# One key buffer with the global keys woven in: window scores as 32 matmuls of 128 columns instead of 64 of 64, with a new order of operations

## The chip, the core and the metric

The kernel runs on one core of one Trainium2 chip. TensorE (PE) multiplies, with its weight loads shown apart as PEld; VectorE (DVE), ScalarE (ACT) and GpSimd (POOL) do the elementwise work; SyncE (SP) issues almost all DMAs. The metric is device time in microseconds (us), the median of several executions.

## The reference

Local and global attention for 8 batches of 8 heads, then a feed-forward network whose activation is h - tanh(h). Everything is float32.

```python
s_g   = scale * q_g @ k_all.T                 # 32 global queries see all 32 + 512 keys
out_g = softmax(s_g) @ v_all
s_ll  = scale * q_l @ k_l.T                   # 512 local queries, head_dim 64
s_ll  = where(abs(i - j) <= 32, s_ll, -1e9)   # a window of 32 to each side
s_lg  = scale * q_l @ k_g.T                   # and all 32 global keys
out_l = softmax([s_lg, s_ll]) @ [v_g, v_l]
x     = concat(out_g, out_l)                  # (8 * 544, 512)
h     = x @ w_in                              # 512 -> 2048
out   = (h - tanh(h)) @ w_out                 # 2048 -> 512
```

The window is cut into blocks of 32 positions: a block of 32 queries needs its own key block, its two neighbours and the 32 global keys, together 128 keys.

## The kernel before

Heads go in pairs (rows 0 to 63 and 64 to 127 of the partitions). Pairs 0 to 7 (batches 0 and 1) use an older scheme (`Pair`). Pairs 8 to 31 (batches 2 to 7, 24 pairs) use `WindowPair`, which the change touches. Each feed-forward product is three float32r products (high x high, high x low, low x high), 512 columns each: hidden steps at L1176 and output steps at L1224, 12 matmuls each; they make up most of PE's work, and attention is threaded between them. The last batch's feed-forward work has a form of its own (L1550, L1576, L1670).

For one window pair the steps are these, with the line of the instruction. Keys and queries come by 8 DMAs (L838) in a form that DVE's 32x32 transposes turn (L842 keys, L845 queries). `scores` (L867) does, for each of 16 blocks and 2 heads, two matmuls of 64 columns: one on the first two key blocks, one on the third key block and the global keys, which lie behind the 512 local columns of the same buffer, `win_kw` (its tile is printed as `first_m`). A float32 matmul is two records in the profile, each with a weight load, so a visit of `scores` shows 128 matmul records. `global_scores` (L889) takes the global queries against all keys, with 8 matmuls of 128 columns and 8 of 64, in all 32 records. Then DVE takes maxima (L967), ACT does the exponentials (L975), POOL the normalization (L989), and DVE turns the probabilities into keys-by-queries (L1007, L956). `product` (L1037, 56 records) multiplies them with the values, which SP has loaded as window slices: four DMAs per pair (L1085, L1086), each window's 96 local rows above the 32 global rows. The product is split into a high and a low part (L368 CAST to `x_hi`, L1070 to `x_lo`) for the feed-forward network.

One visit on PE glues the products of pair j to the scores of pair j+1. The global scores of a pair stand ahead of its scores in time: right after the scores of pair j+1 the buffer `win_kw` is free, DVE turns the keys of pair j+2 into it, and L889 of pair j+2 follows.

The order on every engine is not written out: `Order.run` is a list scheduler that plays the program with durations of its own and picks the operation that can start first, with due times and penalties from the table `CFG`; where an operation may run on two engines (`either`: DVE or ACT), the table's penalties decide. In gaps that it foresees between 5 and 72 us it puts matmuls with no use (`fill`, L1832).

## Time and profile before

| | us |
|---|---|
| median of 3 runs | 943.48 |
| lowest and highest run | 943.43 and 944.66 |
| span of the profiled execution, first to last instruction | 942.0 |
| PE busy in it | 922.5 (98%) |
| DVE, ACT, POOL busy in it | 702.5, 367.2, 342.8 |

The profile is read from PE outwards: with PE busy for 98% of the span, an edit counts by what it takes from PE's own sequence or from the few places where PE stands still. Until about 58 us PE does only attention of the first batch, then both kinds of work, from 184 us the window pairs between feed-forward steps, and from about 811 us the last feed-forward work alone. Busy time of PE hides short losses, because the ends of matmuls are modelled; so the start times in the timeline are read as well.

### The profile page before, as it was taken

The page shows a single profiled execution, that of the slowest core. Times are in us where ns is not written, and L with a number is a line of the kernel's source. Part 1 is how long each engine was busy: PE and PEld are TensorE (multiplying, and loading weights), DVE is VectorE, ACT ScalarE, POOL GpSimd, SP SyncE. Part 2 cuts the span into 40 slices and gives each one's busy share as a digit, 9 for nine tenths or more (in the row PEclk, how much of TensorE's full clock was granted, in tenths as well). Part 3 has the DMA queues.
Part 4 walks back from the last instruction along what each step waited for, and adds up shares of the span by engine and source line. Part 5 has one row for each costly group of instructions (what it writes and reads, how often), then busy time and mean ns, then how long its engine had stood idle before and what let it go on. Part 6 is the DMA issues. An engine that isn't in the chain of part 4 may idle for free.

```text
span 942.0 us, 24357 instructions
## 1 busy us (share of the span) xinstructions
PE 922.5 (98%) x9387; PEld 754.8 (80%) x9387; DVE 702.5 (75%) x2281; ACT 367.2 (39%) x1075; POOL 342.8 (36%) x573
## 2 busy tenths in 40 slices
PE   8989999999999999999999999999999999999998
PEld 5667777778878888888788888888878888899896
DVE  6997565597878876888677778886877786878773
ACT  6976656433334122332324222332223222533232
POOL 4677655543333333334324243333333233110000
PEclk9999999999999999999999999999999999999999
DMA  9565244542344224342424323343434210100001
GB/s 233 151 184 166 85 129 101 96 94 43 69 84 98 55 42 73 70 101 49 78 46 114 57 34 59 74 97 58 74 63 100 49 28 14 46 1 1 1 1 67
DMA packets 243571, 70.25 MB, mean 75 GB/s; under 512 B 228096, under 2 KB 236800, under 8 KB 243456
## 3 DMA queue, kind: packets, MB, share of 16 engines
q1 hardware_dynamic: 242112, 68.19, 33.0%
q8 instruction: 73, 1.20, 0.6%
q10 hardware_dynamic: 1344, 0.52, 0.2%
q14 instruction: 42, 0.34, 0.1%
HBM read 59.77 MB, written 8.91 MB: 73 GB/s over the span
## 4 chain that ended last, share of the span: by engine, by line
PE 91%; DVE 3%; ACT 2%; issue 1%; POOL 1%; DMA 1%; ACTq 0%; POOLq 0%; SPq 0%; DVEq 0%
PE bank L1224 33%; PE bank L1176 32%; PE bank L1550 7%; PE bank L1670 5%; PE bank L1037 5%; PE bank L867 4%; PE bank L889 1%; PE bank L641 1%; PE bank L1576 1%; PE bank L738 1%; DMA first_raw<-in_k_l_dram 1%; PE bank L545 1%; POOL wraw L779 0%; DMA first_raw<-in_q_l_dram 0%; PE bank L661 0%
## 5 line engine op out<-in xcount | busy, mean ns | idle before, releaser
L1193 POOL TENSOR_TENSOR glo<-t,ghi 128x512 fp32r<-128x512 f32 x112 | 145.7, 1301 | 286.0 <-PE bank L1224 192.8
L1007 DVE STREAM_TRANSPOSE keys_first<-prob 32x256 f32<-32x256 f32 x384 | 167.3, 436 | 10.3 <-POOL prob L989 4.0
L1184 ACT ACTIVATE t<-bank 128x512 f32<-128x512 f32 x112 | 66.7, 596 | 226.9 <-PE bank L1176 223.7
L1187 DVE TENSOR_TENSOR t<-bank,t 128x512 f32<-128x512 f32 x112 | 76.8, 688 | 70.2 <-ACT t L1184 69.0
L1224 PE MATMUL bank<-w_out_hi,ghi 128*128 128x512 f32 x448 | 127.2, 397 | 0.2
L1224 PE MATMUL bank<-w_out_hi,glo 128*128 128x512 f32 x448 | 125.4, 394 | 0.0
L1224 PE MATMUL bank<-w_out_lo,ghi 128*128 128x512 f32 x448 | 125.0, 393 | 0.3 <-POOL w_out_lo L451 0.3
L1176 PE MATMUL bank<-x_hi,w_in_hi 128*128 128x512 f32 x448 | 121.7, 393 | 0.3 <-DVE x_hi L368 0.3
L1176 PE MATMUL bank<-x_hi,w_in_lo 128*128 128x512 f32 x448 | 120.4, 391 | 0.0
L1176 PE MATMUL bank<-x_lo,w_in_hi 128*128 128x512 f32 x448 | 120.2, 390 | 0.0
L975 ACT ACTIVATE prob<-prob,st 128x128 f32<-128x128 f32 x192 | 74.5, 391 | 92.1 <-DVE st L967 92.1
L1224 PEld LDWEIGHTS bank<-w_out_hi,ghi 128*128 128x128 f32 x448 | 82.5, 188 | 20.7 <-ACT wpair L368 1.2
L1176 PEld LDWEIGHTS bank<-x_hi,w_in_hi 128*128 128x128 f32 x448 | 83.1, 188 | 19.9 <-issue 1.0
L1176 PEld LDWEIGHTS bank<-x_lo,w_in_hi 128*128 128x128 f32 x448 | 83.9, 188 | 17.7
L1224 PEld LDWEIGHTS bank<-w_out_lo,ghi 128*128 128x128 f32 x448 | 83.2, 188 | 18.6 <-POOL w_out_lo L451 0.7
L1176 PEld LDWEIGHTS bank<-x_hi,w_in_lo 128*128 128x128 f32 x448 | 83.7, 188 | 17.7 <-issue 0.2
L1224 PEld LDWEIGHTS bank<-w_out_hi,glo 128*128 128x128 f32 x448 | 82.8, 188 | 18.2 <-POOL w_in_lo L451 0.2
L989 POOL TENSOR_SCALAR prob<-prob,st 128x128 f32<-128x128 f32 x192 | 68.7, 377 | 47.7 <-DVE st L982 39.4
L368 ACT CAST ghi<-t 128x512 fp32r<-128x512 f32 (+1 forms) x70 | 42.7, 610 | 89.3 <-PE bank L1224 73.3
L1037 PEld LDWEIGHTS bank<-keys_first,values 128*64 128x64 f32 x672 | 42.1, 138 | 8.5 <-DVE t L1187 4.9
L1037 PE MATMUL bank<-keys_first,values 128*64 128x32 f32 (+2 forms) x672 | 46.7, 228 | 0.0
L1037 PE MATMUL bank<-keys_first 128*64 128x32 f32 (+2 forms) x672 | 46.7, 228 | 0.0
(246 smaller groups left out, 1482.9 us busy)
## 6 DMA issues: line engine op xcount, KB each, us to landing
values<-in_v_l_dram SPq DMA_DIRECT2D x24, 336.0 KB, 4.4
keys_first<-in_v_l_dram SPq DMA_DIRECT2D x24, 336.0 KB, 5.3
out_dram<-wpair SPq DMA_DIRECT2D x28, 256.0 KB, 2.1
rawkq<-in_q_l_dram SPq DMA_DIRECT2D x96, 64.0 KB, 2.3
rawkq<-in_k_l_dram SPq DMA_DIRECT2D x96, 64.0 KB, 2.4
first_q<-in_moe_w_in_dram SPq DMA_DIRECT2D x6, 512.0 KB, 4.4
stage<-in_moe_w_out_dram SPq DMA_DIRECT2D x6, 512.0 KB, 3.5
stage<-in_moe_w_in_dram SPq DMA_DIRECT2D x6, 512.0 KB, 4.6
```

What stands on the lines that cost most here:

```text
L368: (nc.scalar.copy if e == "A" else nc.vector.tensor_copy)(dst, src)
L975: nc.scalar.activation(x, x, AF.Exp, bias=s[:, k:k + 1], scale=-1.0, accum_out=s[:, 8 + k:9 + k])
L989: nc.gpsimd.tensor_scalar(x, x, s[:, k:k + 1], 1.0, op0=ALU.mult, op1=ALU.mult)
L1007: nc.vector.transpose(view(win_kf[W * k:W * k + W], [(CH, 2), (P, NT), (1, W)], 3 * G + W * i), src)
L1037: nc.tensor.matmul(dst, win_values[h][:, window(b)], src, start=n == 0, stop=n == len(parts) - 1, skip_group_check=True)
L1176: nc.tensor.matmul(self.h[s][:, j * n:(j + 1) * n], w[:, cc, f * P:(f + 1) * P], self.x()[xi][:, cc, :n], start=part == 0 and cc == 0 and ...
L1184: nc.scalar.activation(tt_[q], self.h[s], AF.Tanh)
L1187: nc.vector.tensor_sub(tt_[q], self.h.pop(s), tt_[q])
L1193: eng[e].tensor_sub(gg[q][1], tt_[q], f32(gg[q][0]))
L1224: nc.tensor.matmul(self.acc[tt], g[:, j * self.n + tt * P:j * self.n + (tt + 1) * P], low_out(f) if wi else high_out(f), start=s == 0 and ...
L1550: nc.tensor.matmul(self.hold(tt, tags), g(), low_out(f) if wi else high_out(f), start=first and k < len(tts), stop=last and k == len(mms) - 1)
L1670: nc.tensor.matmul(dst[:, at], w, m, start=fresh and n == 1, stop=n == 6, skip_group_check=True)
```

## The change

A global key block is stored behind every third local block of `win_kw`, five copies in all (`pos(k) = k + k // 3`). Any three neighbouring key blocks then lie, with one copy of the global keys, in four neighbouring blocks of 32 columns, and a block's scores are one matmul of 128 columns. What follows from it:

- the keys are turned in two steps (480 columns spread out, then 32), and a new copy (`common`) puts the five global blocks in place, on DVE or ACT as the scheduler picks;
- the order of the four blocks within a window now depends on the window's number modulo 3. The values must stand in the same order, so they are loaded in three phases per head: 8 DMAs per head, 16 per pair, with the same bytes. Masks and the lists of `product` follow (the same number of matmuls and the same sizes);
- the table `CFG` has new numbers, from which the scheduler makes another order.

```diff
+    def pos(k):
+        return k + k // 3
...
-                    for last in range(2):
-                        for i in range(4):
-                            b = 4 * t + i
-                            c = W * window(b) + 2 * W * last
-                            o = t * P + 2 * W * last
-                            for h, x in enumerate(t_):
-                                r = slice(64 * h, 64 * h + 64)
-                                keys = view(kw[r], [(g - c, 2), (1, W)], c) if last else kw[r, c:c + 2 * W]
-                                nc.tensor.matmul(x[W * i:W * i + W, o:o + 2 * W], q[r, W * b:W * b + W], keys,
+                    for i in range(4):
+                        b = 4 * t + i
+                        c = W * pos(window(b))
+                        for h, x in enumerate(t_):
+                            r = slice(64 * h, 64 * h + 64)
+                            nc.tensor.matmul(x[W * i:W * i + W, t * P:t * P + P], q[r, W * b:W * b + W], kw[r, c:c + P],
...
-                nc.vector.transpose(win_kw[:, :S], raw[0])
+                nc.vector.transpose(view(win_kw, [(P, 5), (1, 96)]), raw[0][:, :480])
+                nc.vector.transpose(win_kw[:, 640:672], raw[0][:, 480:512])
+
+            def common(e, _):
+                copy(e, view(win_kw, [(P, 5), (1, G)], 96), view(win_gk[self.b % 2][:, self.jj], [(0, 5), (1, G)]))
...
+            add(either(160, "gk"), common, self.after(-3.0), r=[("gkq", self.b % 2)], w=["wg"], ...)
...
-                    nc.sync.dma_start(win_values[h][:96], bass.AP(v.tensor, v.offset, [[D, 96], [W * D, NB - 2], [1, D]]))
-                    nc.sync.dma_start(win_values[h][96:], bass.AP(g.tensor, g.offset, [[D, G], [0, NB - 2], [1, D]]))
+                    for x in range(3):
+                        n = (NB - x) // 3
+                        dst, rows = win_values[h][:, x::3], W * (3 - x)
+                        nc.sync.dma_start(dst[:rows], bass.AP(v.tensor, v.offset + W * D * x, [[D, rows], [3 * W * D, n], [1, D]]))
+                        nc.sync.dma_start(dst[rows:rows + G], bass.AP(g.tensor, g.offset, [[D, G], [0, n], [1, D]]))
+                        if x:
+                            nc.sync.dma_start(dst[rows + G:], bass.AP(v.tensor, v.offset + W * D * 3, [[D, W * x], [3 * W * D, n], [1, D]]))
...
-    CFG = dict(win=-100.0, a_g=0.7314, a_kg=2.7836, a_ph=2.671, a_qs=2.1456, a_w=0.2133, a_wn=0.6018, a_xg=7.3446, d_g=1.3367, d_gl=1.6793,
+    CFG = dict(win=-466.5653, a_g=1.5262, a_kg=1.4158, a_ph=0.7742, a_qs=2.9873, a_w=0.3174, a_wn=0.0, a_xg=7.3446, d_g=1.972,
```

What the new order moves is shown at three places. In the rows below a line number, the instruction, its output and inputs by tile name and the output's size are given; lines of the changed kernel are shifted (L867 is L873, L889 is L894, L1176 is L1186, L1224 is L1234).

On PE, at the start of the window pairs (about 188 us before), between the global scores of the first and the second window pair. Before, the last matmul of the one and the first of the other:

```order
L889 MATMUL bank_98<-first_m,win_gq 32x64
L1224 MATMUL bank_104<-w_out_hi_1525,ghi_70 128x512
L1224 MATMUL bank_104<-w_out_lo_1536,ghi_70 128x512
L1224 MATMUL bank_104<-w_out_hi_1525,glo_71 128x512
L1224 MATMUL bank_102<-w_out_hi_1525,ghi_70 128x512
L1224 MATMUL bank_102<-w_out_lo_1536,ghi_70 128x512
L1224 MATMUL bank_102<-w_out_hi_1525,glo_71 128x512
L889 MATMUL bank_100<-first_m,win_gq 32x2x64
```

Now, from the middle of that stretch to its end:

```order
L1186 MATMUL bank_100<-x_hi_107,w_in_hi 128x512 x4
L1186 MATMUL bank_100<-x_lo_108,w_in_hi 128x512 x4
L1186 MATMUL bank_100<-x_hi_107,w_in_lo 128x512 x4
L1234 MATMUL bank_104<-w_out_hi,glo_73 128x512
L1234 MATMUL bank_105<-w_out_hi,glo_73 128x512
L1234 MATMUL bank_102<-w_out_hi,glo_73 128x512
L1234 MATMUL bank_103<-w_out_hi,glo_73 128x512
L1234 MATMUL bank_104<-w_out_hi,ghi_70 128x512
L1234 MATMUL bank_105<-w_out_hi,ghi_70 128x512
L1234 MATMUL bank_102<-w_out_hi,ghi_70 128x512
L1234 MATMUL bank_103<-w_out_hi,ghi_70 128x512
L894 MATMUL bank_98<-first_m,win_gq 32x2x64
```

Six feed-forward matmuls stood between the two global scores; now 28 do (8 more of L1234 stand ahead of the rows shown).

On DVE, right after a product in the steady stretch: the split of the product into `x_hi` and `x_lo`, then the first maximum of the next pair (L967, printed as ISA). Before:

```order
L368 CAST x_hi_107<-bank_100 128x256
L1070 TENSOR_TENSOR x_lo_108<-bank_100,x_hi_107 128x256
L1074 COPY xg<-bank_100 128x32
L368 CAST x_hi_107<-bank_101 128x256
L1070 TENSOR_TENSOR x_lo_108<-bank_101,x_hi_107 128x256
L1072 TENSOR_TENSOR xg<-bank_101,xg 128x32
L967 ISA prob,st_94<-bank_98,wraw_2020 128x128
```

Now on DVE, and behind it what stands on ACT at the same place:

```order
L1075 TENSOR_TENSOR x_lo_108<-bank_100,x_hi_107 128x256
L1079 COPY xg<-bank_100 128x32
L1075 TENSOR_TENSOR x_lo_108<-bank_99,x_hi_107 128x256
L1077 TENSOR_TENSOR xg<-bank_99,xg 128x32
L961 STREAM_TRANSPOSE keys_first<-pg 128x2x96
L972 ISA prob,st_93<-bank_98,wraw_2007 128x128
```

```order
L936 ACTIVATE pg,st_93<-pg,st_93 128x192 x2
L367 CAST x_hi_87<-bank_99 128x256
L367 CAST x_hi_87<-bank_100 128x256
L367 COPY first_m<-first_m 128x5x32
L980 ACTIVATE prob,st_93<-prob,st_93 128x128 x4
```

The two casts went from DVE to ACT (44 of the 62 `x_hi` casts on DVE did), and `common` (the COPY of 5x32) stands behind them on ACT, in all 24 pairs.

On SP, the loads that follow a product. Before:

```order
L1252 DMA out_dram<-wpair 128x512 x4
L1085 DMA values<-in_v_l_dram 96x14x64
L1086 DMA values<-in_v_g_dram 32x14x64
L1085 DMA keys_first<-in_v_l_dram 96x14x64
L1086 DMA keys_first<-in_v_g_dram 32x14x64
L838 DMA rawkq<-in_k_l_dram 32x16x32 x4
L838 DMA rawkq<-in_q_l_dram 32x16x32 x4
```

Now, the values of one of the two heads (those of the other, `keys_first`, follow in the same way, and then the same eight loads of keys and queries):

```order
L1093 DMA values<-in_v_l_dram 96x5x64
L1094 DMA values<-in_v_g_dram 32x5x64
L1093 DMA values<-in_v_l_dram 64x5x64
L1094 DMA values<-in_v_g_dram 32x5x64
L1096 DMA values<-in_v_l_dram 32x5x64
L1093 DMA values<-in_v_l_dram 32x4x64
L1094 DMA values<-in_v_g_dram 32x4x64
L1096 DMA values<-in_v_l_dram 64x4x64
L1093 DMA keys_first<-in_v_l_dram 96x5x64
```

Sixteen value DMAs stand where four stood, ahead of the keys and queries. Over the whole program the feed-forward matmuls between two visits of the scores number 73 to 120 before and 76 to 116 now (six stretches have 76, seven 80, two 84); changes between feed-forward and attention matmuls, from the first hidden step on, are 140 before and 132 now; and the matmuls with no use are 93 before and 80 now.

## Rows read from the trace of the kernel before

**Rows 1.** The page: engines, and TensorE's clock in tenths.
```profile
PE 922.5 (98%) x9387; PEld 754.8 (80%) x9387; DVE 702.5 (75%) x2281; ACT 367.2 (39%) x1075; POOL 342.8 (36%) x573
PEclk9999999999999999999999999999999999999999
```
**Rows 2.** Windows: stretch, us, busy us of PE, PEld, DVE, ACT, POOL; clock; DMA share, GB/s.
```profile
300.00:350.00 50.00, 49.98 (x568) 40.75 (x567) 39.45 (x136) 14.38 (x48) 18.45 (x32) 1.00 0.35 69
```
**Rows 3.** Timeline of PE, an undisturbed score visit: start us, us, instruction.
```profile
432.77 1.49 PE L867 MATMUL bank<-first_m,hi 64*32 64x64 f32 x128
434.18 1.20 PE L1224 MATMUL bank<-w_out_hi,glo 128*128 128x512 f32 x4
435.22 0.39 PE L1176 MATMUL bank<-x_hi,w_in_hi 128*128 128x512 f32 x1
```
**Rows 4.** One line, 432.77 to 433.03 us: records, ns min/median/max.
```profile
L867 PE MATMUL bank<-first_m,hi x32: 216/216/240, 432.8 to 433.0; 64*32 64x64 f32 x32
```
**Rows 5.** The same for L889, 418.39 to 418.62.
```profile
L889 PE MATMUL bank<-first_m,win_gq x16: 269/281/293, 418.4 to 418.6; 64*32 64x128 f32 x16
```
**Rows 6.** Timeline of PE, a visit of the global scores.
```profile
418.39 0.56 PE L889 MATMUL bank<-first_m,win_gq 64*32 64x128 f32 x32
418.88 0.50 PE L1176 MATMUL bank<-x_hi,w_in_hi 128*128 128x512 f32 x1
```
**Rows 7.** Waits of PE in all: us, times, longest.
```profile
PE bank L867 <- issue: 4.5, 5, 1.2
```
**Rows 8.** Timeline of PE, one of the five score visits with an issue wait.
```profile
277.73 1.42 PE L867 MATMUL bank<-first_m,hi 64*32 64x64 f32 x120
280.28 0.32 PE L867 MATMUL bank<-first_m,hi 64*32 64x64 f32 x8 [1.13 <-issue]
280.52 1.20 PE L1224 MATMUL bank<-w_out_hi,glo 128*128 128x512 f32 x4
```
**Rows 9.** DMA queues: packets, MB, share; whole span, then 277.8 to 278.8 us.
```profile
q8 instruction: 73, 1.20, 0.6%
...
q8 instruction: 1, 0.02, 5.5%
```
**Rows 10.** Timeline of PE between the first two global scores.
```profile
189.25 0.40 PE L1224 MATMUL bank<-w_out_hi,glo 128*128 128x512 f32 x1
190.65 0.56 PE L889 MATMUL bank<-first_m,win_gq 64*32 64x128 f32 x32 [1.00 <-DVE first_m L842]
```
**Rows 11.** Groups by line on DVE: busy us, mean ns, idle before.
```profile
L842 DVE STREAM_TRANSPOSE first_m<-rawkq 128x512 f32<-128x512 f32 x24 | 16.6, 690 | 0.6 <-DMA rawkq<-in_k_l_dram 0.6
L956 DVE STREAM_TRANSPOSE keys_first<-pg 128x192 f32<-128x192 f32 x48 | 16.4, 360 | 19.4 <-PE bank L1037 15.6 <-POOL pg L936 3.8
L368 DVE CAST x_hi<-bank 128x256 fp32r<-128x256 f32 x62 | 25.4, 409 | 10.4 <-PE bank L738 7.3 <-PE bank L1037 3.0
```
**Rows 12.** Timeline of SP behind a product, then one line's issue times and landing.
```profile
515.94 1.94 SPq L838 DMA_DIRECT2D rawkq<-in_k_l_dram  x4
...
L1086 SPq DMA_DIRECT2D keys_first<-in_v_g_dram x24: 677/1410/3256, 176.9 to 774.9; - x24
DMA to landing us min/median/max: 3.7/5.1/6.2
```
**Rows 13.** Timeline: DVE's last turns of a pair; its product and the next scores on PE; chain, 24 feed-forward matmuls.
```profile
293.67 3.19 DVE L1007 STREAM_TRANSPOSE keys_first<-prob 32x256 f32<-32x256 f32 x7
...
298.01 0.30 PE L1037 MATMUL bank<-keys_first,values 128*64 128x96 f32 x1
...
299.89 0.64 PE L867 MATMUL bank<-first_m,hi 64*32 64x64 f32 x40
...
242.66 5.44 PE bank L1176 x24
```

**Rows 14.** Timeline: PE behind another score visit; DVE's last turns of that pair.
```profile
537.18 0.73 PE L1224 MATMUL bank<-w_out_hi,glo 128*128 128x512 f32 x2
...
552.78 4.53 DVE L1007 STREAM_TRANSPOSE keys_first<-prob 32x256 f32<-32x256 f32 x10
```

More of the change, by code (lines that the diff above doesn't have):

```diff
@@ L281 @@
     prob = [probs[t // 2][:, t % 2 * KC:t % 2 * KC + 256] for t in range(NT)]
-    first_m = cp.tile([P, S + 2 * P], F32, name="first_m", tag="hl")
+    first_m = cp.tile([P, S + 160 + 2 * P], F32, name="first_m", tag="hl")
     win_kw = first_m
@@ L773, in fn @@
                     for n in range(3):
-                        x, k = m[rows, W * n:W * n + W], window(b) + n
+                        k = window(b) + n
+                        c = W * (pos(k) - pos(window(b)))
+                        x = m[rows, c:c + W]
                         if abs(k - b) > 1:
@@ L784, in ends @@
             nc.vector.memset(win_gmask(), 0.0)
-            for rows, lo, hi in ((0, 3, 4), (1, 3, 4), (3, 0, 3), (3, 4, 6)):
+            for rows, lo, hi in ((3, 0, 2), (2, 3, 6), (0, 4, 5), (1, 4, 5)):
                 nc.vector.memset(win_gmask()[W * rows:W * rows + W, W * lo:W * hi], BIG)
@@ L848, in add_load @@
                 add(("S", 2.2), load(a, src), self.after(-14.0), w=[("raw", "kq")[a]], xfer=1.46)
-            add(("D", 0.69), keys, self.after(-3.0), r=["raw"], w=["ww"], res=["fm", "gl0"] if self.j == H else [])
+            add(either(160, "gk"), common, self.after(-3.0), r=[("gkq", self.b % 2)], w=["wg"], res=["fm", "gl0"] if self.j == H else [])
+            add(("D", 0.84), keys, self.after(-3.0), r=["raw"], w=["ww"], res=["fm", "gl0"] if self.j == H else [])
             add(("D", 0.69), queries, self.after(-3.0), r=["kq"], w=["hk0"])
@@ L874, in global_scores @@
             names = [("sg", self.j, h) for h in range(2)]
-            kw, q, g = win_kw, win_gq[self.b % 2][:, self.jj], self.gcol
+            kw, q = win_kw, win_gq[self.b % 2][:, self.jj]
             def mm(e, tags):
                 t_ = self.box["g"] = [bank([P, NG_], tags[n]) for n in names]
-                for x_, n, dims in ((0, 4 * W, [(6 * W, 2), (3 * W, 2), (1, W)]), (1, 2 * W, None)):
+                for last in range(2):
                     for c in range(4):
@@ L883, in mm @@
                             at = x[W * c:W * c + W]
[L884 to L888 removed]
+                            if last:
+                                out, keys = at[:, 2 * W:4 * W], view(kw[r], [(17 * W, 2), (1, W)], W * c)
+                            else:
+                                out, keys = view(at, [(4 * W, 2), (1, 2 * W)]), view(kw[r], [(5 * W, 2), (4 * W, 2), (1, W)], W * (4 + c))
                             nc.tensor.matmul(out, q[r], keys, start=True, stop=True, tile_position=(64 * h, W * c),
                                              skip_group_check=True)
[L892 removed]
+            return dict(fn=mm, d=0.45, names=names, r=["ww", "wg", ("gkq", self.b % 2)], res=[f"pg{self.u}{h}" for h in range(2)] + ["pg0", "pg1", "pl0", "pl1"] * (self.j < H + 2),
                         rows=1.0, ldw=0.03, tail=0.1, mode="s")
```

61 lines of the change are left out of this document (27 added, 34 removed).

## The prediction

> **What bounds the kernel now.** The page first: PE is busy for 98% of the span, and its clock row shows 9 in all forty slices, the upper of the two levels (2.4 GHz) throughout [rows 1]. DVE comes next with 75%. The table by stretches says the same of the steady part: in 50 us PE is busy for 49.98 and DVE for 39.45 [rows 2]. So time can come only from PE's own sequence, or from the few places where PE stands still. Busy time is no measure of these, since the ends of matmuls are modelled (the group of a score visit is shown with 1.49 us, and the next instruction starts 1.41 us after it [rows 3]). I therefore read the timeline by starts. Its unit is a feed-forward matmul: 24 in 5.44 us, 0.227 us each [rows 13]. Then I read PE's waits (the one to see is "issue", 4.5 us in five waits, all at the scores [rows 7]), the timeline around one of them [rows 8], and last DVE and SP, to see what could become late.
>
> **The scores.** An undisturbed visit of the scores takes 434.18 - 432.77 = 1.41 us for 128 records [rows 3]. Its first 32 records end issuing within 0.27 us, 8.4 ns each [rows 4]; the other 96 and the run-out take 1.14. The changed visit has 64 records of 128 columns with the same tile of 64 rows and 32 columns. The trace has this shape in the global scores: 16 such records in 0.24 us, 15.0 ns each [rows 5]; with 16 of 64 columns behind them the visit takes 0.49 us [rows 6]. At 8.4 ns, the latter are 0.13, so the run-out is 0.12. The new visit is 64 x 15.0 ns + 0.12 = 1.08 us; the 15.0 contain a slow first group, without which some 14 remain and the visit is 1.02. I take 1.05. Each visit saves 0.36 us, and 24 visits **8.6 us**, all on the path, as PE works before and behind them.
>
> The rows show that columns alone do not set the time: 8.4 ns for 64 columns early in a visit [rows 4], but (1.41 - 0.12 - 0.27) / 96 = 10.6 ns for the same later [rows 3], as if records then came no faster. That is half of the saving. The other half is that 15.0 ns is less than twice 8.4. The Trainium skill speaks against it: "TensorE: Matmul & The Clock Gate", section "Step-by-step: what each phase is for", says that throughput is purely N cycles. By that rule 128 x 64 columns are as long as 64 x 128 and the change of shape is worth nothing; the trace doesn't agree within a visit, as said, but the rule is kept as the first rival.
>
> **The issue waits.** In the stalled visit 120 records run as usual, then PE stands for 1.13 us, and the visit is 280.52 - 277.73 = 2.79 us instead of 1.41, so 1.38 are lost where the row shows 1.13 [rows 8]. Five such waits, 4.5 us by the row [rows 7], are thus 4.5 + 5 x 0.25 = 5.8. What is waited for: queue q8 brings instructions, 73 packets of 16,384 bytes in all (1.20 MB), and one of them lies beside the wait [rows 9]. PE has 9387 records and as many weight loads, 18,774 instructions [rows 1], or 257 for each packet; so I read a packet as 256 instructions of 64 bytes of PE. A score visit is 128 records and 128 loads, a whole packet used in about 1.3 us, which no other place of the kernel does: 256 feed-forward instructions take 128 x 0.227 = 29 us. When a packet ends early in a visit, the next one, asked for only then, seems late. After the change a visit holds 128 instructions. With the product ahead of it (56 records, 112 instructions, 299.89 - 298.01 = 1.88 us [rows 13]) 240 instructions take 1.88 + 1.05 = 2.9 us, and any 256 reach into feed-forward work and take over 4. The wait's own end, at about 2.5 us from the visit's start [rows 8], bounds how long a packet takes. All five should go: **5.8 us**. Next late is nothing that the rows show.
>
> The Trainium skill ("Runtime: NRT & Kernel Launch", section "Instruction fetch mechanics") has blocks of 16 KiB, 256 instructions, fetched while the ones before run, the crossing mostly hidden. The size agrees with the packets; that it is hidden doesn't where the issue waits lie on crossings. If they had another cause, they could stay: the second rival.
>
> **The second global scores.** At the start of the window pairs PE starts a matmul at 189.25 and the global scores only at 190.65; they wait for DVE's turn of the keys [rows 10]. The start should come 0.227 later, so 1.2 us are lost. Six feed-forward matmuls stand between the two global scores before, 28 after: 22 x 0.227 = 5.0 us of cover more. Gain **1.2 us**.
>
> **Changes of kind and unused matmuls.** Four feed-forward matmuls behind a visit take 435.22 - 434.18 = 1.04 us instead of 0.91 [rows 3], 0.13 for the change; 140 changes become 132: **1.0 us**. Of matmuls with no use there are 13 fewer. They stand in gaps that the planner foresees, so I count nothing; the nearest row has 0.227 us for a matmul [rows 13], which makes 2.9 us at most, for the low end. I bound them on the other side by nothing, as fewer instructions in the same sequence give no loss.
>
> **What it adds, and what hides it.** *DVE.* The keys' turn was 512 columns in 0.690 us, and 192 columns take 0.360 [rows 11]: 0.166 fixed and 1.03 ns a column. 480 and 32 are 0.66 + 0.20 = 0.86, 0.17 more, 4.1 us in 24 pairs. Against that 44 of the casts of 0.409 us [rows 11] leave DVE, 18 us. ACT gets them, and the 24 copies of the global keys (160 columns, below the 0.36 of the nearest row, so under 9 us); it is busy for 39% [rows 1]. The chain from the scores through maxima, exponentials and turns to the product hides these. In a pair with only 73 feed-forward matmuls (before the change the shortest, 17.5 us from 280.52 [rows 8] to 298.01 [rows 13]) DVE's last turn ends at 293.67 + 3.19 = 296.86, 1.15 us early, after 16.3 us. The shortest stretches after the change have 76 matmuls, 17.2 us; with the global scores' 0.49 and the run-outs (0.13 each) some 18.1 us stand between scores and product. I take zero. If the cover is gone, each microsecond of lateness is paid in those stretches.
>
> *SP.* Values take 16 DMAs per pair, not 4, with the same bytes. The cover is the time from one product to the next, 1.05 + 18.1 = 19.2 us at the least. An issue costs 0.49 us by the key loads behind (1.94 for four) and 1.41 as the median of the last of the four value loads [rows 12]. I take 0.49: the long one has to push through the descriptors of all four, and those don't grow. Then 7.8 us, and landing 5.1 to 6.2 [rows 12], 14 in all, 5 less than the cover. Queued behind are the 8 loads of keys and queries for the pair after, 4 us more, which DVE wants only after the next scores. At 1.41 it would be 22.6 + 5.1: late, the fourth rival. Masks, queries and the product keep their sizes: nothing.
>
> **Sum.** 8.6 + 5.8 + 1.2 + 1.0 = 16.6 us. The profiled span of 942.0 becomes 925.4; the median lies 1.4 above the span (943.48), taken as unchanged: **926.9 us**.
>
> **Rivals.** 1. *The shape gives nothing*: time goes by columns, and a visit stays at 1.41 us. For it: equal columns. Against: 8.4 against 10.6 ns within one visit. 926.9 + 8.6 = 935.5.
>
> 2. *The issue waits stay*, five of them at the same price wherever packets end. For it: they are only placed by count, and other places could be late as well. Against: all five stand in score visits [rows 7], which halve. 926.9 + 5.8 = 932.7.
>
> 3. *The softmax chain is late* in the short stretches. Its length isn't fixed: in a long stretch it runs from 537.18 to 552.78 + 4.53 = 557.31, 20.1 us [rows 14], as DVE does feed-forward work between. After the change the casts and the copy of the global keys stand on ACT around the exponentials, a hop more, and DVE's order is new. If short stretches took 20.0 us, six of 76 would lose 1.9 each and seven of 80 (0.9 us longer) 1.0: 18 us, 945 in all; half of it, likelier, gives 936. Against it: 16.3 us where the stretch is short, and 14 us less work on DVE.
>
> 4. *Slower: the values come late.* Sixteen issues on one queue, as a small DMA's issue has a fixed part that counts by number. It decides from 19.2 - 5.1 = 14.1 us, 0.88 us an issue. At 1.0 the loads land after 21.1, which loses 1.9 in each of six stretches, 1.0 in seven and 0.1 in two, 18.6 us: 926.9 + 18.6 = 945.5, slower than before. For it: the median of 1.41 [rows 12]; against: 0.49 for loads of similar make beside it.
>
> **How the numbers follow.** The forecast has 0.62, the first rival 0.10, the second 0.08, the third 0.11 (half of it with 936 and less), the fourth 0.05, mixtures and what I don't see 0.04. The low end: visits of 1.02 (0.7 us), the unused matmuls (2.9), 0.3 for the runs' scatter: 923.0. The high end goes to the first rival, 935.5, and takes in the second. The forecast's own range is 923.0 to 930.0. Outside remain about 0.15. A measurement of this kernel can tell about 0.2% from no change. Faster by more than that: 0.62 + 0.10 + 0.08 + 0.09 of the third and 0.03 of the rest, 0.92; the same 0.02; slower 0.06.
>
> **What would show it.** In the changed profile: a visit of the scores from start to next start of 1.02 to 1.08 us (at 1.41 the first rival holds); no issue wait of PE at the scores, though still some 73 packets less 24 x 128 / 256 = 12; no wait ahead of the second global scores; the last turns of DVE ending before each product, and PE's waits at the product none (else the third); the value loads landing before the product, with a mean issue near 0.5 us (else the fourth); DVE's busy time lower by about 14 us and ACT's higher by more. Wrong would be the whole if PE showed a lower clock, or if a wait of several microseconds stood at a place where PE is continuous now.

## The result and the profile after

| | before | after |
|---|---|---|
| median, us | 943.5 | 928.37 (927.57 to 928.72) |
| span of the profiled execution, us | 942.0 | 926.9 |
| ratio | | 0.9834, 95% interval 0.9821 to 0.9848 |

The change takes 15.1 us off the span; 16.6 were forecast, 928.4 stands where 926.9 was predicted, inside the range. (The ratio is worth 15.7 us of 943.5; its interval, some 1.3 us to each side, holds both values.) The page of the changed kernel has these lines, to be held against [rows 1] and [rows 9]:

```profile
PE 912.6 (98%) x7838; PEld 744.7 (80%) x7838; DVE 695.1 (75%) x2244; ACT 393.7 (42%) x1145; POOL 345.4 (37%) x588
...
PEclk9989999999999999999999999999999999999999
...
q8 instruction: 62, 1.02, 0.5%
```

PE is as full as before, with 1549 records fewer (1536 in the scores, 13 unused ones), and 11 packets of instructions fewer come in. One slice of the clock row, around 46 to 70 us, shows 8 where all were 9. Of PE's waits, as us in total, times, longest, one is new at the scores:

```profile
PE bank L873 <- DVE first_m L847: 0.7, 1, 0.7
```

The "issue" wait of [rows 7] is gone, and so is the wait of the second global scores [rows 10]. The new one stands before the first scores (L873). A visit of the scores, and the start behind it, in the timeline of PE:

```profile
423.27 1.16 PE L873 MATMUL bank<-first_m,hi 64*32 64x128 f32 x64
424.35 1.21 PE L1186 MATMUL bank<-x_hi,w_in_hi 128*128 128x512 f32 x4
```

From start to next start it is 1.08 us, against 1.41 in [rows 3].

Where the 15.1 us come from, summed over PE's starts (the time from one record to the next, put down to the line of the first), in the two profiled executions:

| | forecast | measured |
|---|---|---|
| scores, all 24 visits: 39.96 us before, 25.90 after | 8.6 + 5.8 = 14.4 | 14.1 |
| wait before the second global scores: 1.17 gone; before the first scores: 0.89 new | 1.2 | 0.3 |
| rest of the feed-forward matmuls (two gaps near 181 us among them, 0.9) | 1.0 | 2.3 |
| everything else, nearly all of it pairs 0 to 7, ahead of the first hidden step (58.5 us before, 60.2 after) | 0 | -1.6 |

### The profile page after: what moved, and what is told of

Same layout as the page of the kernel before. It is cut to its first block, busy times and chain, and to the rows that moved or that the text cites. A ratio compares the mean times of both kernels' runs of the same rounds, so it can differ in the third digit from the quotient of the medians.

```text
span 926.9 us, 21769 instructions
## 1 busy us (share of the span) xinstructions
PE 912.6 (98%) x7838; PEld 744.7 (80%) x7838; DVE 695.1 (75%) x2244; ACT 393.7 (42%) x1145; POOL 345.4 (37%) x588
## 4 chain that ended last, share of the span: by engine, by line
PE 94%; DVE 2%; DMA 2%; POOL 1%; ACT 0%; issue 0%; SPq 0%; ACTq 0%; DVEq 0%; POOLq 0%
PE bank L1234 34%; PE bank L1186 33%; PE bank L1560 7%; PE bank L1680 6%; PE bank L1042 5%; PE bank L873 3%; PE bank L640 1%; PE bank L894 1%; PE bank L737 1%; PE bank L1586 1%; DMA rawkq<-in_k_l_dram 1%; PE bank L660 1%; PE bank L544 1%; DMA first_raw<-in_q_l_dram 0%; DMA wpair<-in_moe_w_out_dram 0%
## 5 line engine op out<-in xcount | busy, mean ns | idle before, releaser
L1234 PE MATMUL bank<-w_out_hi,glo 128*128 128x512 f32 x448 | 125.5, 394 | 0.0
L1234 PE MATMUL bank<-w_out_lo,ghi 128*128 128x512 f32 x448 | 124.7, 392 | 0.0
L1234 PE MATMUL bank<-w_out_hi,ghi 128*128 128x512 f32 x448 | 124.5, 392 | 0.0
L1186 PE MATMUL bank<-x_hi,w_in_hi 128*128 128x512 f32 x448 | 123.3, 397 | 0.3 <-DVE x_hi L367 0.3
L1186 PE MATMUL bank<-x_hi,w_in_lo 128*128 128x512 f32 x448 | 120.3, 391 | 0.0
L1186 PE MATMUL bank<-x_lo,w_in_hi 128*128 128x512 f32 x448 | 120.3, 390 | 0.0
L1186 PEld LDWEIGHTS bank<-x_hi,w_in_hi 128*128 128x128 f32 x448 | 82.2, 188 | 21.4 <-DVE xg L1077 2.0
L1186 PEld LDWEIGHTS bank<-x_lo,w_in_hi 128*128 128x128 f32 x448 | 84.0, 188 | 18.1 <-issue 0.2
L1186 PEld LDWEIGHTS bank<-x_hi,w_in_lo 128*128 128x128 f32 x448 | 83.8, 188 | 18.0 <-issue 0.2
L1234 PEld LDWEIGHTS bank<-w_out_lo,ghi 128*128 128x128 f32 x448 | 83.2, 188 | 18.6 <-issue 0.7
L1234 PEld LDWEIGHTS bank<-w_out_hi,glo 128*128 128x128 f32 x448 | 82.8, 188 | 19.1 <-issue 1.5
L1234 PEld LDWEIGHTS bank<-w_out_hi,ghi 128*128 128x128 f32 x448 | 83.3, 188 | 18.2 <-issue 0.5
L367 ACT CAST ghi<-t 128x512 fp32r<-128x512 f32 (+1 forms) x76 | 46.5, 612 | 98.4 <-PE bank L1234 81.1
```

Source lines behind the costliest of these rows:

```text
L367: (nc.scalar.copy if e == "A" else nc.vector.tensor_copy)(dst, src)
L1186: nc.tensor.matmul(self.h[s][:, j * n:(j + 1) * n], w[:, cc, f * P:(f + 1) * P], self.x()[xi][:, cc, :n], start=part == 0 and cc == 0 and ...
L1234: nc.tensor.matmul(self.acc[tt], g[:, j * self.n + tt * P:j * self.n + (tt + 1) * P], low_out(f) if wi else high_out(f), start=s == 0 and ...
```

## Experiments

Each ratio below is to the kernel before, run beside it on the same chip. Its median there was 944.8 us for two64, shift64, old_order and casts_dve, 944.4 for old_stores, values32, keys_ahead and more_fill, and 943.9 for after_again, spread and best (the names stand with the results below). So ratios are compared, and 0.001 is 0.94 us.

### The shape alone undone

```diff
-                        c = W * pos(window(b))
-                            nc.tensor.matmul(x[W * i:W * i + W, t * P:t * P + P], ..., kw[r, c:c + P], ...)
+                    for last in range(2):
+                            c, o = W * pos(window(b)) + 2 * W * last, t * P + 2 * W * last
+                                nc.tensor.matmul(x[W * i:W * i + W, o:o + 2 * W], ..., kw[r, c:c + 2 * W], ...)
```

> The changed kernel with its new layout and order, but each block's scores as two matmuls of 64 columns again. Theory (records and instructions count): a visit goes from 1.08 us back to 1.41, 24 x 0.33 = 7.9 us; and with 256 instructions in a visit the issue waits return. If packets of 256 instructions end where counting puts them, four visits have a packet's end at their instructions 206 to 252 (those that start about 211, 445, 608 and 711 us in the changed kernel) and wait about 1.2 us each: 4.8 us more, 928.4 + 12.7 = 941. Rival (columns count): the same columns, 928.4. Rival (issue waits have another cause): 936.3 without any wait at the scores.

Measured (two64): 940.8 us, 0.9959 (0.9947 to 0.9972), 11.8 us above the changed kernel's ratio, where 12.7 were expected. Layout, order, loads and copies are those of the changed kernel; only the matmuls differ. PE's wait, and the timeline of one visit:

```profile
PE bank L874 <- issue: 5.3, 6, 1.3
```
```profile
450.11 1.40 PE L874 MATMUL bank<-first_m,hi 64*32 64x64 f32 x119
452.61 0.32 PE L874 MATMUL bank<-first_m,hi 64*32 64x64 f32 x9 [1.10 <-issue]
452.86 1.20 PE L1187 MATMUL bank<-x_hi,w_in_hi 128*128 128x512 f32 x4
```

Eighteen visits take 1.41 us again (one of them, the first, 1.32), and six wait: those at 208.6, 276.6, 345.0, 450.1, 615.8 and 720.8 us. Four of them are the four named ahead, by place in the program (211, 445, 608 and 711 us in the changed kernel); the other two are those for which the count gave 204, just under the 206 taken as the limit. So time does not go by columns, and the issue waits come with the number of instructions.

### The packets' ends moved

```diff
+    extra = [32]
     def fill(n, j):
...
+        for _ in range(min(4, extra[0])):
+            extra[0] -= 1
+            nc.tensor.matmul((bank([P, KC], j) if isinstance(j, int) else j)[:, :8], masks[1][:, :P], masks[1][:, :8], start=True, stop=True)
```

> The kernel before with 32 small matmuls of 8 columns (64 instructions with their weight loads) added within the first 60 us, in places where PE waits; nothing else is changed. Theory (an issue wait is a late packet of 256 instructions, and comes where a packet ends between instructions 206 and 252 of a score visit): the waits leave the visits at about 207, 278, 457, 642 and 694 us and come to those at about 327, 386, 510 and 564 us, four instead of five; the sum of excess falls from 6.0 to some 4 us, the time to 941 to 943. Rival (the waits belong to what else happens at those places, such as transfers): the same five visits wait, 943.5.

Measured (shift64): 946.7 us, 1.0022 (1.0013 to 1.0032). Two visits that stood at one place in both kernels, near 457 us and near 510 us of the kernel before, here in the timeline of the shifted kernel:

```profile
459.33 1.48 PE L867 MATMUL bank<-first_m,hi 64*32 64x64 f32 x128
460.74 0.96 PE L1224 MATMUL bank<-w_out_hi,ghi 128*128 128x512 f32 x3
...
510.66 1.33 PE L867 MATMUL bank<-first_m,hi 64*32 64x64 f32 x110
513.03 0.41 PE L867 MATMUL bank<-first_m,hi 64*32 64x64 f32 x18 [1.03 <-issue]
513.37 0.50 PE L1224 MATMUL bank<-w_out_hi,ghi 128*128 128x512 f32 x1
```

The first had a wait of 1.4 us before and has none (1.41 from start to start); the second had none and takes 2.71 us. All four visits that were named wait (327.4, 387.8, 510.7 and 565.8 us); two more wait for 0.5 to 0.7 us, at 748.9, where the count gives 204, and at 209.2, where it gives 182, outside the limits of the theory. Of the five that waited before, four run in 1.41 us now. Thirty-two matmuls of 8 columns at the other end of the program decide which visit waits, so it is the count of instructions and nothing that happens beside it. The traces show it more sharply still. If every matmul, weight load and semaphore instruction of PE is counted from the start, the first late matmul of each of the seventeen waiting visits (five in the kernel before, six in two64, six here) has the same count modulo 256, that of 209.2 too: all begin at the end of a packet. Every visit with such an end behind 204 or more of its instructions waits, sixteen in all; behind 182 one waits, and four others with 182 to 186 don't. The time was misjudged: the scores' sum fell only from 40.0 to 39.4 us, as six visits wait; the 32 matmuls, with what PE stands still between them, take 3.0 us; and two more issue waits, of 0.4 us each, stand outside the scores (at L889 and L1176), at the same count modulo 256.

### The shape without the new order

> The changed kernel with the table of numbers of the kernel before: the new shape without the new order. Theory (the shape carries nearly all): visits of 1.08 us save 7.9, the five issue waits go, 5.8, so about 929.8 (928.5 to 931.5), and the clock stays up near 50 us as before. Rival (the new order carries the gain): 935 or more.

The edit is the table `CFG` of the kernel before in the changed kernel. Measured (old_order): 939.0 us, 0.9946 (0.9925 to 0.9968). The expectation was missed by 9 us: the visits save 12.6 us of PE's time (27.4 for all), no issue wait is left, and yet the kernel is only 5 us faster than before. PE, ACT and SP show where it went. PE's waits; its timeline near 509 us; ACT's; and SP's, where the sixteen value loads are cut to the first and the last:

```profile
PE bank L1235 <- ACT wpair L368: 4.1, 6, 1.3
```
```profile
508.27 0.61 PE L1235 MATMUL bank<-w_out_hi,ghi 128*128 128x512 f32 x2
509.74 0.50 PE L1235 MATMUL bank<-w_out_hi,ghi 128*128 128x512 f32 x1 [0.86 <-ACT wpair L368]
...
500.26 1.28 ACT L368 COPY wpair<-bank 128x512 f32<-128x512 f32 x2 [1.45 <-PE bank L1235]
...
509.10 0.59 ACT L368 COPY wpair<-bank 128x512 f32<-128x512 f32 x1 [3.33 <-DMA out_dram<-wpair]
...
497.15 0.31 SPq L1094 DMA_DIRECT2D values<-in_v_l_dram  x1
...
506.04 0.60 SPq L1097 DMA_DIRECT2D keys_first<-in_v_l_dram  x1
506.74 1.02 SPq L1263 DMA_DIRECT2D out_dram<-wpair  x2
```

Read from below: two output rows are copied out at 500.26 to 501.5 us, but their stores are issued at 506.74, behind sixteen value loads that hold SP from 497.15 on. Once a store has read its buffer, ACT can copy the next rows (509.10), and only then is the accumulator's bank free for PE (509.74). Four value loads hold SP for 3.4 us in the kernel before (509.77 to 513.12), not 9.5; behind four, the store could go out some 6 us earlier, as soon as its rows are copied (an estimate from these rows). The rival's sentence, that the new order carries the gain, is right in its number, but the cause could be tried directly:

### The stores ahead of the value loads

```diff
+            def later(e, _):
+                held.append((load, e))
-            add(("S", 8.0), load, self.after(10.0), w=["vh"], ...)
+            add(("S", 8.0), later if self.j + 2 < len(pairs) else load, self.after(10.0), w=["vh"], ...)
...
                 def fn(e, _):          # the loads of the next keys and queries
+                    while held:
+                        f, x = held.pop()
+                        f(x, None)
```

> The changed kernel with the table of the kernel before (as old_order), and on SP each pair's sixteen value loads issued only when the next loads of keys follow, so behind the two stores of outputs that stood behind them near 507, 612 and 717 us. Theory (what old_order lost is SP's queue: sixteen value loads ahead of a store keep the store's buffer from ACT's copy, and PE's output steps wait for that copy): the six waits of PE on ACT's copy into wpair, 4.1 us, go; 4 to 5 us less than old_order, 0.990 of the kernel before. Rival (ACT is late by itself, from the casts or the order): the waits stay, 0.9946.

Measured (old_stores): 931.6 us, 0.9865 (0.9850 to 0.9880), 7.6 us less than the kernel it was made from, where 4 to 5 were expected. Between the two profiled executions it is 6.0 us; 5.2 of them stand at the feed-forward matmuls, and 1.0 ahead of the first hidden step, where the two programs don't differ. The stores go out at 500.55, the value loads behind them, and the wait of PE on ACT's copy is gone; ACT's own wait for the stores, 13.6 us in nine waits in old_order, is down to the last row:

```profile
500.55 1.05 SPq L1271 DMA_DIRECT2D out_dram<-wpair  x2
501.69 0.41 SPq L1099 DMA_DIRECT2D values<-in_v_l_dram  x1
```
```profile
ACT wpair L368 <- DMA out_dram<-wpair: 2.5, 3, 1.5
```

So the shape with the old table brings 12.7 us of the 15.7 (0.0135 of 0.0166) as soon as SP's queue lets it. The new order's main share, then, seems to be that it puts all four stores of a batch ahead of a pair's value loads; SP's order in the changed kernel has the four together there in every batch but the first. No run takes this alone out of the new order. The remaining 2.9 us between this kernel and the changed one were not taken apart.

### Twice as many value loads

```diff
                     for x in range(3):
-                        n = (NB - x) // 3
-                        dst, rows = win_values[h][:, x::3], W * (3 - x)
+                        for lo, n in ((0, 2), (2, (NB - x) // 3 - 2)):
+                            dst, rows, s = win_values[h][:, x + 3 * lo:x + 3 * (lo + n) - 2:3], W * (3 - x), 3 * W * D * lo
```

> The changed kernel with each value load cut in two by windows: 32 DMAs per pair with the same bytes. The 16 take 10.3 us on SP now, 0.64 each with the long ones. Theory (an issue costs by its number, and the cover is some 19 us from product to product): about 20 us of issue; values land 2.3 us later, so in the stretches of 76 and 80 matmuls they come 2 to 4 us late, thirteen times: 928.4 + 20 to 45, near 960. Rival (the issue goes by bytes and descriptors): some 10 us still, no change, 928.4.

Measured (values32): 993.9 us, 1.0508 (1.0480 to 1.0535). The price of an issue was as expected, the loss was not, and its path was another. The 32 issues of one pair hold SP for 19.7 us (328.67 to 348.33), 0.61 each with half the bytes, where sixteen took 0.64 each: an issue costs by its number. But the time is 64 us above the changed kernel's by the ratios, not 20 to 45. PE's waits and one of ACT's:

```profile
PE bank L1186 <- DVE xg L1079: 18.6, 5, 5.2
PE bank L1234 <- ACT wpair L367: 11.5, 5, 10.6
PE bank L873 <- DVE first_m L847: 9.5, 1, 9.5
PE bank L1042 <- DMA keys_first<-in_v_l_dram: 7.5, 8, 2.0
```
```profile
ACT wpair L367 <- DMA out_dram<-wpair: 49.9, 11, 16.6
```

Of these only the last of PE's rows, 7.5 us, are values that come late for a product. What is queued behind the values costs as much or more: keys (L873), stores (L1234), and whatever stands behind a DVE or ACT that waits. The granted clock falls with it, to a mean of 0.965 over the 994.7 us of the span: that is some 70 us at 0.50, the lower of the two levels, where PE's matmuls take twice their time. The expectation had no term for this; it can be up to some 35 us of the loss (an estimate, half of the 70).

### The keys of the first window pair ahead of its values

The new wait before the first scores has the same cause. The changed kernel's SP, DVE and PE:

```profile
182.06 0.60 SPq L1096 DMA_DIRECT2D keys_first<-in_v_l_dram  x1
182.76 2.14 SPq L842 DMA_DIRECT2D rawkq<-in_k_l_dram  x4
...
186.70 0.68 DVE L846 STREAM_TRANSPOSE first_m<-rawkq 128x480 f32<-128x480 f32 x1 [3.27 <-DMA rawkq<-in_k_l_dram]
187.30 0.17 DVE L847 STREAM_TRANSPOSE first_m<-rawkq 128x32 f32<-128x32 f32 x1
...
186.40 0.39 PE L1234 MATMUL bank<-w_out_hi,glo 128*128 128x512 f32 x1
187.52 1.13 PE L873 MATMUL bank<-first_m,hi 64*32 64x128 f32 x63 [0.73 <-DVE first_m L847]
```

The keys are issued behind sixteen value loads (173.3 to 182.7 us) and are turned too late: the scores start 0.9 us later than they could behind the matmul of 186.40.

```diff
+            if self.j == H:
+                self.values, load = load, lambda e, _: None
...
+                    if self.j == H and a == 0:      # behind the four loads of this pair's keys
+                        self.values(e, _)
```

> The changed kernel with one thing moved on SP: the first window pair's keys are loaded ahead of its sixteen value loads, not behind. Theory (the first scores, which start 0.9 us late at 187.5 us, wait for keys that were queued behind 9.4 us of value loads): the wait of the first scores goes, 0.7 to 0.9 us less, 927.6 where the changed kernel has 928.4. Rival (the keys' buffer is free too late anyway): no change.

Measured (keys_ahead): 932.6 us, 0.9878 (0.9864 to 0.9893): 4 us slower than the changed kernel. The theory was right about the wait and wrong about the time. PE, SP and PE's windows (us, busy us of PE, PEld, DVE, ACT, POOL, granted clock, DMA share, GB/s):

```profile
184.31 0.39 PE L1238 MATMUL bank<-w_out_hi,glo 128*128 128x512 f32 x1
184.63 1.16 PE L875 MATMUL bank<-first_m,hi 64*32 64x128 f32 x64
...
190.20 1.47 PE L1238 MATMUL bank<-w_out_hi,ghi 128*128 128x512 f32 x2 [3.40 <-ACT wpair L367]
...
176.52 0.42 SPq L1095 DMA_DIRECT2D values<-in_v_l_dram  x1
...
185.99 1.02 SPq L1266 DMA_DIRECT2D out_dram<-wpair  x2
```
```profile
185.00:190.00 5.00, 1.80 (x90) 1.27 (x70) 3.86 (x28) 0.44 (x1) 0.00 (x0) 0.95 0.56 161
190.00:195.00 5.00, 4.80 (x11) 3.54 (x12) 1.71 (x5) 4.91 (x21) 2.58 (x5) 0.50 0.49 140
```

The first scores start without a wait. But the keys' loads had to wait for their buffer until 174.35, so that the sixteen value loads behind them begin at 176.52 instead of 173.31 us. The two stores behind these go out 1.0 us later than in the changed kernel (185.99, not 184.99), and PE waits 3.4 us for their buffer. Behind that wait the granted clock is 0.50, the lower of the two levels (1.2 GHz), for more than 5 us: the matmuls that follow take about twice their time, which is what the wait costs on top of its own length.

The 4 us are less than what the edit costs in this execution. The matmul ahead of the first scores starts at 184.31 us, 2.1 us sooner than the 186.40 of the changed kernel, though up to the loads near 174 us the two programs are the same. The next section shows where that comes from.

### The slow stretch near 50 us

The 8 in the clock row is a stretch at the lower level. Windows of the kernel before (first two rows) and of the changed kernel:

```profile
45.00:50.00 5.00, 3.73 (x49) 3.18 (x48) 4.40 (x18) 3.57 (x14) 4.81 (x8) 1.00 0.65 216
50.00:55.00 5.00, 4.71 (x71) 3.56 (x67) 4.92 (x19) 4.12 (x11) 3.60 (x5) 1.00 0.34 79
```
```profile
45.00:50.00 5.00, 2.88 (x40) 2.37 (x41) 4.80 (x19) 3.61 (x12) 4.81 (x8) 0.88 0.23 60
50.00:55.00 5.00, 5.00 (x36) 3.31 (x34) 2.92 (x5) 3.14 (x9) 2.47 (x5) 0.50 0.74 195
```

PE was busy for 2.9 us of the five, and then runs at 0.50 for the next five. The profile of keys_ahead, the same program up to about 174 us, has the same windows thus:

```profile
45.00:50.00 5.00, 2.95 (x45) 2.21 (x45) 4.80 (x20) 4.03 (x15) 4.81 (x9) 1.00 0.26 78
50.00:55.00 5.00, 4.86 (x66) 4.11 (x68) 4.68 (x13) 3.82 (x10) 3.52 (x4) 1.00 0.71 195
```

PE was busy for as little, and the clock did not fall. The stretch comes in most executions of this head, not in all: of eight executions of the changed kernel seven have a mean clock of 0.996 or 0.997 and one 0.999, of 31 of the kernel before two have 0.997 or 0.998 and the others more. The profiles of casts_dve and spread show 1.00 and 0.66 in the two windows, a shorter stretch. With and without it, the two executions above differ by the 2.1 us just named. The edit that is to prevent it:

```diff
-        if not self.FILL[0] <= free < self.FILL[1] or s - free < 0.9:
+        if not self.FILL[0] <= free < self.FILL[1] or s - free < 0.6:
-        n = int((s - free - 0.4) * 0.7 * rate / 0.0945)
+        n = int((s - free - 0.3) * 1.0 * rate / 0.0945)
```

> The changed kernel with 36 more matmuls of no use, in the gaps of the first 72 us that the planner foresees (116 in all, not 80). Theory (the granted clock of 0.50 between 50 and 55 us, which the kernel before doesn't have, comes from PE being busy for only 2.9 of the 5 us ahead of it, and costs about 1 us): the clock stays at 1.00 there, 0.5 to 1 us less, 927.6. Rival (the waits there set the time and the slow clock is hidden, or the fill delays what follows): no change or slower.

Measured (more_fill): 927.8 us, 0.9824 (0.9809 to 0.9838), 0.9 us under the changed kernel's ratio; the intervals overlap. The clock stayed up as expected, and not by chance: all nine executions with these matmuls (four here, five of best below) have a mean clock of 0.999 or 1.000. The gain is less than the slow stretch costs. The one execution of the changed kernel with 0.999 took 927.57 us, as little as this one, and in the profile of more_fill the matmul ahead of the first scores starts at 185.08 us, 0.8 later than in that of keys_ahead: the added matmuls take time too. The windows of more_fill:

```profile
45.00:50.00 5.00, 4.40 (x62) 3.78 (x60) 4.77 (x18) 4.10 (x13) 4.41 (x7) 1.00 0.34 101
50.00:55.00 5.00, 4.48 (x50) 3.50 (x50) 4.68 (x16) 3.89 (x12) 3.67 (x6) 1.00 0.74 195
```

### The casts back on DVE

```diff
             def high(e, _):
-                copy(e, places()[0], self.box["o", half][:, l0:l0 + 256])
+                copy("D", places()[0], self.box["o", half][:, l0:l0 + 256])
```

> The changed kernel with the 40 casts of the window pairs' products back on DVE, at the places where they stood on ACT; the order is otherwise the same. DVE's last turns end only 0.3 to 0.5 us before the product in seven stretches of 80 matmuls, and once after its start. Theory (the chain over DVE is nearly on the path in the short stretches, so moving the casts to ACT was needed): each pair's chain starts or runs 0.3 to 0.8 us later, some 8 products wait up to 0.5 us, 930 to 933. Rival (hidden, as the forecast's zero says): 928.4.

Measured (casts_dve): 928.2 us, 0.9827 (0.9812 to 0.9842), no different from the changed kernel. The rival holds. (The expectation's count was off: five of the seven stretches of 80, not all, have their last turn 0.3 to 0.5 us ahead of the product.) In the stretch of 80 matmuls that begins near 424 us, DVE's first maximum comes 0.4 us after the next feed-forward matmul (424.76 and 424.35) in the changed kernel, and 1.0 us after it (425.68 and 424.64) here, so the chain does start later; but its last turns end as close to the product as before. Last turns and product of the changed kernel, then of this one:

```profile
441.14 1.83 DVE L1012 STREAM_TRANSPOSE keys_first<-prob 32x256 f32<-32x256 f32 x4
...
443.46 0.30 PE L1042 MATMUL bank<-keys_first,values 128*64 128x96 f32 x1
```
```profile
441.39 1.83 DVE L1012 STREAM_TRANSPOSE keys_first<-prob 32x256 f32<-32x256 f32 x4
...
443.72 0.30 PE L1042 MATMUL bank<-keys_first,values 128*64 128x96 f32 x1
```

A margin of 0.5 us between a chain's end and its product is thus no measure of the slack inside the chain: 0.6 us at its start were swallowed on the way.

### The first window pair's queue in another order

The queue of the first window pair can be laid out so that neither its keys nor the stores come last: its keys, eight of its value loads, the two stores, the other eight.

```diff
+                    if self.j == H and a == 0:
+                        self.values(e, _, (0,))
+                        held.append([2, lambda: self.values(e, _, (1,))])
...
                             nc.sync.dma_start(out[row:row + hi - lo, :], y[lo:hi])
+                        if held:
+                            held[0][0] -= 1
+                            if not held[0][0]:
+                                held.pop()[1]()
```

> The changed kernel once more, unaltered, as the measure for the two runs beside it: 0.983 to 0.984 of the kernel before.

> The changed kernel with SP's queue of the first window pair in another order: the pair's keys, eight value loads, the two stores of outputs, the other eight value loads. Loading the keys first (keys_ahead) let the first scores start at 184.6 instead of 187.5 us, but the two stores then went out behind all sixteen value loads, at 186.0, and an output step of PE waited 3.4 us for their buffer. Theory (only the queue's order is in the way): the stores go out near 182 us, PE waits for neither, and 2 to 3 us of the changed kernel's time go: 0.981 of the kernel before. Rival (something else is late by then, as DVE's turns for the second pair): within 0.5 us of the changed kernel.

> The queue's order of spread and the 36 unused matmuls of more_fill together. If the two are independent (one stands near 185 us, the other near 50 us), the sum of both: 3 to 4 us less than the changed kernel, 0.980 of the kernel before. If the first waits only move the second ones, no more than spread alone.

Measured: the changed kernel again (after_again) 928.2 us, 0.9833 (0.9820 to 0.9847); spread 927.2 us, 0.9823 (0.9810 to 0.9837); best 926.5 us, 0.9815 (0.9802 to 0.9828). In spread the stores are issued at 183.07 and the scores start right behind the matmuls ahead of them:

```profile
185.86 0.39 PE L1241 MATMUL bank<-w_out_hi,glo 128*128 128x512 f32 x1
186.18 1.16 PE L878 MATMUL bank<-first_m,hi 64*32 64x128 f32 x64
```

The gain is 1.0 us, near the length of the wait, not the 2 to 3 expected: of the 2.9 us by which the scores of keys_ahead stood earlier, 2.1 were the slow stretch near 50 us that its execution didn't have. In the profiled execution of spread that stretch is shorter too, and the matmul ahead of the scores starts at 185.86, 0.5 us sooner than in the changed kernel's; so its lead isn't the queue's alone. With the fill the gain is 1.6 us, near the sum of the two, not the 3 to 4 expected. Each difference is small against its interval, so best against the changed kernel is likely, not certain; against the kernel before it is 17.4 us.

## Why the prediction was right, step by step

**What bounds it.** PE from end to end, before and after: it held, and the sum over PE's starts closes on the span's 15.1 us.

**The scores.** The shape's gain stood as worked out from the rows of the global scores: 1.08 us for a visit against 1.05 taken (1.08 was the first value worked out), so 8.1 us for the 24 visits instead of 8.6. The Trainium skill's rule that throughput is purely N cycles ("TensorE: Matmul & The Clock Gate", "Step-by-step: what each phase is for") does not hold for these small tiles: with equal columns, halving the records took a visit from 1.41 to 1.08, and two64 took it back to 1.41. The first rival fell.

**The issue waits.** All gone, 6.0 us by starts where 5.8 were counted. That they are packets of instructions that come late was an argument before; the two runs that moved the count show it: of their twelve waits in score visits eight were named before they ran, three stand at a count of 204, next to the limit, and one at 182. All twelve begin at the end of a packet; why that one packet was late is open. The Trainium skill ("Runtime: NRT & Kernel Launch", "Instruction fetch mechanics") calls the crossing of a block mostly hidden; here it is, but for 5 of 73 crossings, which cost 6.0 us. The second rival fell. One step of the argument was turned round: a packet that ends early in a visit does no harm (ends behind 2 to 176 of a visit's instructions wait nowhere); it is one that ends late, behind 204 or more, so that the burst has used nearly the whole packet in its 1.4 us. That the waits would go followed from either: the shortest time that the changed kernel takes over one packet's 256 instructions is 5.0 us (counted in its trace), where over 4 was forecast.

**The second global scores.** Here a step failed. Its wait went as forecast, but the step on SP that says of keys and queries queued behind the value loads that DVE wants them "only after the next scores" forgot the first window pair, whose keys have no earlier stretch to come in: 0.9 of the 1.2 us came back as a wait of the first scores.

**Changes of kind and unused matmuls.** 1.0 us forecast; the feed-forward lines lost 2.3 more than the two waits explain, of which 0.9 are two gaps near 181 us that the new order no longer has; the 1.4 that remain are near the forecast, but no run shows the changes of kind by themselves. The unused matmuls are 13 fewer and take 11.8 us as before, so counting nothing was right.

**The head.** The forecast counted nothing for pairs 0 to 7, and the profiled execution loses 1.6 us there. All of it can be the slow stretch near 50 us: between keys_ahead's execution without it and the changed kernel's with it lie 2.1 us in the same sequence, and in the two profiles of this head without it the first hidden step starts at 57.65 (keys_ahead) and 57.37 us (two64), sooner than the 58.48 of the kernel before. So the new order of the head is not slower in itself; it is the clock, which falls in most of its executions, and the forecast had no term for that. "Wrong would be the whole if PE showed a lower clock" had named the sign; by that sentence the forecast failed here, though the number stayed in its range.

**DVE and ACT.** Right where it counted (no product waits), off in size: DVE's busy time fell by 7.4 us, not 14. The casts (62 to 18, 17.9 us) and the keys' turn in two parts (0.68 + 0.17 us, 3.8 more in all) came as worked out (the fixed part of a turn is 0.162 us by the rows, not 0.166); the rest are many small groups. The third rival did not come: in five of the seven stretches of 80 matmuls the last turns end only 0.3 to 0.5 us before the product, and in one of 76 the very last ends after the product's start, but casts_dve shows that this closeness hides slack.

**SP.** The issue was taken as 0.49 us and is 0.6 to 0.65 (10.3 us for sixteen, 299.03 to 309.3). The reason given for 0.49, that the long issue pushes through the descriptors of all four loads, is shown by no run; in values32 the price went by the number of issues. The landing fell from 5.1 to some 2.3 us, so the values are in time and the fourth rival's condition was not met. What the step missed is who else stands in that queue. The value loads were compared with their own cover alone, while the first to be hurt by a longer queue are the stores behind them, through a buffer, ACT's copy and a bank. In the changed kernel the new order keeps these ahead; with the old one the same change would have been worth 5 us instead of 15.7. The forecast met the number partly because the order searched anew avoided a cost that the prediction had not priced.

## What to carry to other kernels

Count instructions as well as columns: where a tile is small, a wider matmul saves time with equal columns, and a burst of 256 instructions of PE in 1.4 us can outrun their supply, while half as many don't. When a change adds DMAs to a queue, price each transfer that stands behind them, stores above all, and follow a store's buffer back to the engine that refills it. And when a layout changes together with a tuned order, run the layout with the old order before crediting either: one queue may be all that lies between them.

## What the runs showed of the hardware

- All seventeen issue waits of score visits begin at the end of a packet of 256 instructions (the same count modulo 256). In a burst of 256 instructions an end behind 204 or more of them always cost 0.5 to 1.7 us, one behind 182 once 0.7 us, and four behind 182 to 186 nothing. Adding 64 instructions 150 us and more ahead moves the waits to other visits.
- With equal columns, 128 records of 64-column float32 matmuls on tiles of 64 rows by 32 columns took 1.41 us, 64 records of 128 columns 1.08 us.
- A wait of PE costs more than its length where the granted clock falls behind it: 3.4 us of waiting was followed by more than 5 us at 0.50. The same head of a program runs with such a stretch in one execution (0.50 from 50 to 55 us) and without it in another (1.00), 2.1 us apart, with PE busy for 2.88 and 2.95 of the 5 us ahead.
- A value load's issue on SP takes 0.64 us from one to the next with four or five windows (16 in 10.3 us) and 0.61 with two or three (32 in 19.7 us).
